# State @ w_in as three float32r passes on split weights, the limit on GpSimd, and another order of the first steps

## The chip, the cores and the metric

One core of one Trainium2 chip runs the whole program. The metric is the device time of one execution in microseconds (us), lower is better. A difference of 0.2% of this kernel, some 2.9 us, is about what its measurement can tell from no change.

## The reference, cut to what matters

```python
# attention between x (8, 8, 512, 64) and state (8, 8, 32, 64), per batch and head
a = softmax(scale * x @ state.T);  xread = a @ state          # 512 rows of a batch
a2 = softmax(scale * state @ x.T); sread = a2 @ x             # 32 rows of a batch
x = concat([xread, sread], rows).reshape(8 * 544, 512)
# first feed-forward, d_ff 2048
h = x @ w_in;  g = maximum(0.01 * h, h);  x = g @ w_out
# second feed-forward, d_ff 1536: silu(x @ w_gate) * (x @ w_val) @ w_out2
```

The weights reach the kernel as 64-bit floats, seen as pairs of 32-bit integers.

## The kernel before

`xread @ w_in` is never computed in that order. For each batch b and block g of 512 hidden columns the kernel makes `state @ w_in` once (32 state rows of each of 8 heads, in sw tiles) and multiplies by the softmax `a`. Exactness comes from splitting: a float32 value v is kept as h, v rounded to float32r (a ScalarE cast, `split_h`, L165), and l = v - h (a VectorE subtraction, `split_l`, L168). A product is then three float32r matmuls, l·h, h·l and h·h, added up in PSUM (`passes`, L437).

The work before the change lies in the first stage of the program, the start and batch 0 (j = 0). In it the 16 pieces of w_in, keys ("in", g, k), and 16 of w_out, keys ("out", f), are loaded (tile ws, 128x512 pairs) and turned into float32 by `convert`, a generator that is pumped one step for each letter c: scale (ScalarE, L214), low (ScalarE, L215), sign (VectorE, L216), limit (VectorE, L219), join (VectorE, L222) and add (VectorE, L225, tile raw or w_in). A piece of w_out is split afterwards into w_parts. A piece of w_in is kept in float32, unsplit, in the tile w_in, and also stored to DRAM.

Two functions use it:

- `product_sw` (L459, letter p): the states of four batches of two heads, `flat`, times one piece of w_in, one head on partitions 0 to 63 and one on 64 to 127, each into its own PSUM bank; ScalarE copies both banks to `sw` (L474) and SP stores them. There are 32 of these, all in the first stage. The letters of batch 0 use the two banks "a" and "b".
- `state_win` (L453, letter h and the steps "keep"): the states of batch 0, two pairs of heads from the tile `states`, into one bank (L456); it is split directly into swh and swl. There are 8.

Both are plain float32 matmuls, which the trace shows as two instructions each. `START` is the order of the first steps written as letters, `SLOT0` that of the 16 slots of batch 0. In a slot, `h_mm` makes a block of hidden columns (six matmuls ps_h), `h_act` its activation and split (hs, gh, gl), and `y_mm` twelve matmuls into ps_y with w_parts. `scores` (ps_s, L319) and the softmax steps (letters 0 and 1) stand in between. All engines run their instructions in the order in which the program issues them, and wait on one another through semaphores.

`place_states` (letters s and S) copies `flat` into the block layout `states` on ScalarE (L1239), batch 0 first, then batches 1 to 7.

Of the kernel before, what the change touches and what calls it, by code (L numbers as in the profile page):

```python
# [25 lines left out]
def kernel(  # L26
# [61 lines left out]

    LOADS = "xswxxwww"
    ORDER = "iiiioiiooiioiioioiioioioiooooooo"  # L90
    START = "spc0Scpccc0p0cpccpcc1ccchcc1cccpc1clcpp0hcccpclp1c01cpcmcc"
    SLOT0 = [
        "DcHcpAccccSYLpcZccc",
        "DcHcAcccpSYLpccZccc",
# [135 lines left out]
    def store(key):  # L230
        if key[0] == "in":
            nc.sync.dma_start(out=win_dram[key[1]][:, key[2], :], in_=raw[key])

    def convert(keys, room, prepare, load_next, finish=None):


        done, before, prev = None, None, None
        todo = list(keys)
        while todo or before or (finish and done):
            key = todo.pop(0) if todo and room(todo[0]) else None  # L240
            if not (key or before or (finish and done)):
# [12 lines left out]
            yield 0.42  # L254
            if key:
                ops["low"]()
                ops["sign"]()
            yield 0.42
            if prev:
                prev["join"]()  # L260
            yield 0.69
            if split:
                finish[1](done)
                ready.append(done)
            if prev:
                prev["add"]()
                load_next()
                if not finish or before[0] == "in":
                    ready.append(before)
                    store(before)  # L270
            yield 0.69
            done, before, prev = before, key, ops

# [173 lines left out]


    WO = {}
    products = []  # L450
    sw_ps, SW_raw, SW = {}, {}, {}

    def state_win(b, g, q, bank):  # L453
        ps = (ps_y if bank == "y" else ps_a).tile([P, 512], F32, tag=bank, name="ps_sw")
        for i in range(2):
            nc.tensor.matmul(  # L456
                ps[2 * NS * i:2 * NS * (i + 1)], lhsT=states[:, 2 * q + i, b, :], rhs=raw["in", g, 2 * q + i],
                start=True, stop=True,
            )  # L459
        return ps  # L460

    def product_sw(g, p, bs, banks):

        pool = ps_y if banks == "yy" else ps_a
        ps = [pool.tile([P, 512], F32, tag=tag, name="ps_sw") for tag in banks]
        for e in range(2):
            half = slice(D * e, D * (e + 1))
            nc.tensor.matmul(  # L468
                ps[e], lhsT=flat[half, p, 4 * bs:4 * bs + 4, :].rearrange("d b n -> d (b n)"),
                rhs=raw["in", g, p][half], start=True, stop=True,  # L470
            )
        staged = stage_sw()
        for e in range(2):
            nc.scalar.copy(staged[e], ps[e])  # L474

            r = slice(NS, P) if bs == 0 else slice(0, P)
            nc.sync.dma_start(out=sw_dram[bs][g][2 * p + e, r], in_=staged[e][r])
# [3 lines left out]
    def stage_sw():  # L481

        if not sw_stages:
            y, x = ab.tile([P, KD, S], F32, tag="yst", name="sw"), first1.tile([P, 2, 512], F32, tag="x_tail", name="sw")
            sw_stages[:] = [[y[:, 0], y[:, 1]], [y[:, 2], y[:, 3]], [x[:, 0], x[:, 1]]] + [
                [pool.tile([P, 512], F32, tag=tag, name="sw", bufs=2) for pool, tag in ((cv, "sw"), (xin, "xn"))]
                for _ in range(2)
            ]
        sw_stages.append(sw_stages.pop(0))
        return sw_stages[-1]  # L490
# [541 lines left out]
    with tc.manual_schedule():  # L1032
# [12 lines left out]
                    src = rows(w_out, key[1])  # L1045
                stage(key, src, cv)

        pair = [None]

        def place1(key):  # L1050

            if key[0] == "in":
                n, half = divmod(KD * key[1] + key[2], 2)
                if half == 0:
                    pair[0] = wres.tile([P, 2, 512], F32, tag=f"wr{n + NF1 // 2}", name="w_in")
                raw[key] = pair[0][:, half, :]
            else:
                raw[key] = cv.tile([P, 512], F32, tag="raw", name="raw", bufs=4)

        def finish1_h(key):  # L1060
            while any((KD * g + p) // 2 + NF1 // 2 == key[1] for g, p, _ in products):
                pump_products(1)
            t = wres.tile([P, 2, 512], F32R, tag=f"wr{key[1]}", name="w_parts")
            WO[key[1]] = (t[:, 0, :], t[:, 1, :])
            split_h(t[:, 0, :], raw[key])

        def finish1_l(key):
            split_l(WO[key[1]][1], raw.pop(key), WO[key[1]][0])


        keys2 = []
# [111 lines left out]
        def keep_steps(g, q):  # L1183
            def product():
                pump_until(("in", g, 2 * q + 1))
                keep_sw_h(g, q, state_win(0, g, q, "b"))

            return [{"P": [product]}, {"D": [lambda: keep_sw_l(g, q)], "cost": 0.6, "now": True}]

# [30 lines left out]
        keep = [(0, 0), (0, 1)]  # L1220
        low = list(keep)

        flat = cv.tile([P, NPAIR, B, NS], F32, name="flat")
# [12 lines left out]
        def place_states(some):  # L1236
            for e in range(2):
                half = slice(D * e, D * e + D)
                nc.scalar.copy(states[half, :, some, NS * e:NS * e + NS], flat[half, :, some])  # L1239

        background[0] = convert(keys1, lambda key: True, place1, next_load1, (finish1_h, finish1_l))

# [3 lines left out]
        for action in START:  # L1246
            if action in "01":
                step = [next(halves[int(action)], {})]
                for part in "DAPL":
                    run(step, part)  # L1250
            elif action == "p":
                pump_products(1, "yy")
            elif action == "h":
                keep_sw_h(*keep[0], state_win(0, *keep.pop(0), "y"))
            elif action == "l":
                keep_sw_l(*low.pop(0))
            elif action == "s":
                place_states(slice(0, 1))
            elif action == "S":
                place_states(slice(1, B))  # L1260
            elif action in "mM":
                f = "mM".index(action)
                if f not in firsts:
                    h_mm(0, f)
                    firsts[f] = h_act(0, f)
                next(firsts[f], None)
            else:
                pump(1)
# [2 lines left out]
                run([step], part)  # L1271
        for g, q in keep:
            pump_until(("in", g, 2 * q + 1))
            keep_sw_h(g, q, state_win(0, g, q, "y"))
        for g, q in low:
            keep_sw_l(g, q)
        for f in range(2):
# [215 lines left out]
```

## Time and profile before

| what | value |
|---|---|
| median of three runs | 1469.8 us (1468.29 to 1470.42) |
| the profiled execution | 1469.83 us, of which the span of its instructions is 1468.0 us |
| PE busy in the span | 98% |
| VectorE (DVE), ScalarE (ACT), GpSimd (POOL) busy in the span | 57%, 47%, 0% |
| PE busy in the first 42 us, and from 42 to 141 us | 27.39 us, 93.78 us |
| PE busy from 141 us on | 1323.15 of 1327 us |

A share of the whole span says little here: the change touches only the part up to about 141 us, where the 16 slots of batch 0 end. At 42 us the first ps_y matmul starts. Those two marks cut the trace into a head, the slots of batch 0, and the rest.

### The profile page before, as it was taken

The numbers are of one execution on the slowest core, as the hardware profiler recorded it, in microseconds if no ns is written. First come the engines' busy times: TensorE is split into PE (matmuls) and PEld (weight loads), VectorE is DVE, ScalarE is ACT, GpSimd is POOL, SyncE is SP. The second block draws the span as 40 slices with busy tenths as digits, with TensorE's granted clock in tenths as the row PEclk, the third lists the DMA queues.
The fourth block names the chain that finished last, engine by engine and source line by source line (L and its number), as shares of the span: only waits on it lengthen the run. The fifth ranks groups of instructions, "written<-read, shape, count | busy, mean of one in ns | idle before, by whom it ended". The sixth has DMA issues, their size and how long they took to land.

```text
span 1468.0 us, 20651 instructions
## 1 busy us (share of the span) xinstructions
PE 1444.3 (98%) x7530; PEld 1153.4 (79%) x7530; DVE 829.5 (57%) x1476; ACT 687.8 (47%) x1243; POOL 3.0 (0%) x8
## 2 busy tenths in 40 slices
PE   6999999999999999999999999999999999999998
PEld 1545777777777778888888888888888888988887
DVE  5877677677767676243454535555344655544442
ACT  6877656655655665454333433334233343333322
POOL 0000000000000000000000000000000000000000
PEclk8999999999999999999999999999999999999999
DMA  8895556665655656360668676667666397876345
GB/s 283 301 319 200 187 198 228 204 222 197 233 204 194 224 194 208 97 198 35 203 199 277 232 235 199 194 220 243 231 193 194 101 321 241 267 251 192 116 153 191
DMA packets 145764, 307.55 MB, mean 209 GB/s; under 512 B 14080, under 2 KB 34816, under 8 KB 144640
## 3 DMA queue, kind: packets, MB, share of 16 engines
q1 hardware_dynamic: 144368, 297.72, 61.7%
q10 hardware_dynamic: 1296, 8.52, 1.4%
q8 instruction: 60, 0.98, 0.3%
q14 instruction: 40, 0.33, 0.1%
HBM read 231.74 MB, written 74.45 MB: 209 GB/s over the span
## 4 chain that ended last, share of the span: by engine, by line
PE 97%; ACT 1%; DVE 1%; DMA 0%; issue 0%; SPq 0%; ACTq 0%
PE ps_y L444 24%; PE ps_o L444 19%; PE ps_x L742 18%; PE ps_h L444 14%; PE ps_s L742 9%; PE ps_a L742 4%; PE ps_sw L468 2%; PE ps_t L444 2%; PE ps_yt L444 2%; PE ps_s L319 1%; PE ps_r L416 1%; PE ps_sw L456 1%; PE ps_a L402 0%; ACT sw L474 0%; DMA flat<-in_dram 0%
## 5 line engine op out<-in xcount | busy, mean ns | idle before, releaser
L444 PE MATMUL ps_y<-gh,w_parts 128*128 128x512 f32 x1024 | 339.3, 391 | 0.0
L742 PE MATMUL ps_x<-yc,wq 128*128 128x512 f32 x1152 | 278.0, 389 | 0.0
L742 PEld LDWEIGHTS ps_x<-yc,wq 128*128 128x128 f32 x1152 | 216.2, 188 | 44.8
L444 PE MATMUL ps_o<-wo,zh 128*128 128x512 f32 x768 | 236.3, 389 | 0.0
L444 PEld LDWEIGHTS ps_y<-gh,w_parts 128*128 128x128 f32 x1024 | 192.2, 188 | 51.7 <-issue 7.6
L444 PE MATMUL ps_y<-gl,w_parts 128*128 128x512 f32 x512 | 199.4, 389 | 0.0
L168 DVE TENSOR_TENSOR gl<-hs,gh 128x512 fp32r<-128x512 f32 (+1 forms) x144 | 95.1, 661 | 141.6 <-ACT gh L165 141.4
L444 PEld LDWEIGHTS ps_o<-wo,zh 128*128 128x128 f32 x768 | 144.2, 188 | 29.8
L550 ACT ACTIVATE hs<-ps_h 128x512 f32<-128x512 f32 (+1 forms) x144 | 82.7, 574 | 172.4 <-PE ps_h L444 168.8
L444 PE MATMUL ps_o<-wo,zl 128*128 128x512 f32 x384 | 149.5, 389 | 0.1
L742 PE MATMUL ps_s<-yc,wq 128*128 128x512 f32 x576 | 146.1, 389 | 0.0
L168 DVE TENSOR_TENSOR zl<-z,zh 128x512 fp32r<-128x512 f32 x96 | 66.4, 691 | 114.6 <-ACT zh L165 114.6
L742 PEld LDWEIGHTS ps_s<-yc,wq 128*128 128x128 f32 x576 | 108.1, 188 | 22.4
L165 ACT CAST zh<-z 128x512 fp32r<-128x512 f32 x96 | 59.3, 622 | 140.7 <-PE ps_o L444 140.6
L762 ACT ACTIVATE sg<-C 128x512 f32<-128x512 f32 x72 | 45.5, 632 | 158.1 <-DVE C L758 158.1
L444 PEld LDWEIGHTS ps_y<-gl,w_parts 128*128 128x128 f32 x512 | 96.1, 188 | 19.6
L444 PE MATMUL ps_h<-ah,swl 128*128 128x512 f32 x256 | 106.3, 415 | 1.1 <-DVE swl L168 1.1
L758 DVE TENSOR_TENSOR C<-ps_s,C 128x512 f32<-128x512 f32 x48 | 33.2, 691 | 122.9 <-PE ps_s L742 122.9
L444 PE MATMUL ps_h<-al,swh 128*128 128x512 f32 x256 | 100.2, 391 | 0.2 <-DVE al L168 0.2
L754 ACT COPY C<-ps_x 128x512 f32<-128x512 f32 x96 | 55.9, 583 | 94.6 <-PE ps_x L742 94.6
L444 PE MATMUL ps_h<-ah,swh 128*128 128x512 f32 x256 | 100.2, 391 | 0.0
L165 ACT CAST gh<-hs 128x512 fp32r<-128x512 f32 (+1 forms) x144 | 85.7, 595 | 3.0
(129 smaller groups left out, 1912.8 us busy)
## 6 DMA issues: line engine op xcount, KB each, us to landing
wo<-wo SPq DMA_DIRECT2D x96, 512.0 KB
wq<-quad_gate SPq DMA_DIRECT2D x168, 256.0 KB
wq<-quad_val SPq DMA_DIRECT2D x168, 256.0 KB
ws<-in_dram SPq DMA_DIRECT2D x68, 512.0 KB
sw<-sw_dram SPq DMA_DIRECT2D x56, 256.0 KB
quad_gate<-hl SPq DMA_DIRECT2D x24, 512.0 KB
quad_val<-hl SPq DMA_DIRECT2D x24, 512.0 KB
yr<-y_dram SPq DMA_DIRECT2D x34, 256.0 KB
```

Of the source, the lines that this page charges most:

```text
L165: nc.scalar.copy(dst, src)
L168: nc.vector.tensor_tensor(out=dst, in0=src, in1=hi.bitcast(F32), op=ALU.subtract)
L319: nc.tensor.matmul(ps[2 * NS * i:2 * NS * (i + 1)], lhsT=states[:, p, b, :], rhs=xt.pop((b, p)), start=True, stop=True,)
L416: nc.tensor.matmul(ps[NS * k:NS * (k + 1), i], lhsT=v["et"][:, n:n + NS], rhs=tokens[i][:, c, NS * k:NS * (k + 1)], start=(c == 0), stop=( ...
L444: nc.tensor.matmul(ps, lhsT=w, rhs=v, start=first and n == 0, stop=last and n == len(todo) - 1)
L456: nc.tensor.matmul(ps[2 * NS * i:2 * NS * (i + 1)], lhsT=states[:, 2 * q + i, b, :], rhs=raw["in", g, 2 * q + i], start=True, stop=True,)
L468: nc.tensor.matmul(ps[e], lhsT=flat[half, p, 4 * bs:4 * bs + 4, :].rearrange("d b n -> d (b n)"), rhs=raw["in", g, p][half], start=True, s ...
L550: nc.scalar.activation(hs, ps[:, :n], AF.Prelu, alpha=0.01)
L742: nc.tensor.matmul(bank, lhsT=a, rhs=v, start=first and n == 0, stop=last and n == len(todo) - 1, skip_group_check=True,)
L754: nc.scalar.copy(t[0], src)
L758: nc.vector.tensor_tensor(out=kept[0], in0=bank, in1=kept[0], op=ALU.add)
L762: nc.scalar.activation(t[0], c, AF.Sigmoid)
```

## The change

Every piece of w_in is now split like w_out, into w_parts, a list `places` assigns it one of twelve places (tags wr4 to wr15, four of them used twice), and a place is overwritten only after all products of the piece in it have been issued (`clear`). The states are split as well: flat_h (ScalarE) and flat_l (VectorE), and for batch 0 first_h and first_l, block layouts filled by GpSimd copies. `product_sw` becomes three float32r passes, each for both heads in turn; `state_win` becomes six full-width passes. The limit of all but the first four pieces moves from VectorE to GpSimd. The copy of the states of batches 1 to 7 moves from ScalarE to GpSimd. A copy of a one-column tile `table` puts ScalarE's table load ahead of the first landing. sw copies have eight staging tiles rather than ten, since the tile x_tail now holds firsts_hl. START is another string; SLOT0 stays.

```diff
-    START = "spc0Scpccc0p0cpccpcc1ccchcc1cccpc1clcpp0hcccpclp1c01cpcmcc"
+    START = "sccccScc0ccc0cpccc10cpccpc1cpc0chc1chpc0lcp1l1mcpcpcc"
...
+        engine = nc.gpsimd if key[0] in ("in", "out") and key not in keys1[:4] else nc.vector
...
-            "limit": lambda: nc.vector.tensor_scalar(
+            "limit": lambda: engine.tensor_scalar(
                 out=hi_f, in0=hi_f, scalar1=HI_MAX, scalar2=-HI_MAX, op0=ALU.min, op1=ALU.max
...
-    def state_win(b, g, q, bank):
+    def state_win(g, q, bank):
+
         ps = (ps_y if bank == "y" else ps_a).tile([P, 512], F32, tag=bank, name="ps_sw")
-        for i in range(2):
-            nc.tensor.matmul(
-                ps[2 * NS * i:2 * NS * (i + 1)], lhsT=states[:, 2 * q + i, b, :], rhs=raw["in", g, 2 * q + i],
-                start=True, stop=True,
-            )
+        passes(
+            [((first_h[:, 2 * q + i], first_l[:, 2 * q + i]), WIN[g, 2 * q + i]) for i in range(2)], ps, True, True
+        )
+        kept.add((g, q))
         return ps
...
-        for e in range(2):
-            half = slice(D * e, D * (e + 1))
-            nc.tensor.matmul(
-                ps[e], lhsT=flat[half, p, 4 * bs:4 * bs + 4, :].rearrange("d b n -> d (b n)"),
-                rhs=raw["in", g, p][half], start=True, stop=True,
-            )
+        wh, wl = WIN[g, p]
+        for n, (st, w) in enumerate(((flat_l, wh), (flat_h, wl), (flat_h, wh))):
+            for e in range(2):
+                half = slice(D * e, D * (e + 1))
+                nc.tensor.matmul(
+                    ps[e], lhsT=st[half, p, 4 * bs:4 * bs + 4, :].rearrange("d b n -> d (b n)"), rhs=w[half],
+                    start=n == 0, stop=n == 2,
+                )
...
+        table = cv.tile([P, 1], F32, name="table")
+        nc.gpsimd.memset(table, 0.0)
+        nc.scalar.copy(table, table)
         nc.gpsimd.memset(states, 0.0)
+        nc.gpsimd.memset(firsts_hl.bitcast(F32), 0.0)
...
+        def split_states():
+            split_h(flat_h, flat)
+            split_l(flat_l, flat, flat_h)
+            for t, of in ((first_h, flat_h), (first_l, flat_l)):
+                for p in range(NPAIR):
+                    for e in range(2):
+                        half = slice(D * e, D * e + D)
+                        c = NS * (2 * (p % 2) + e)
+                        nc.gpsimd.tensor_copy(out=t[half, p, c:c + NS], in_=of[half, p, 0])
...
             elif action == "S":
-                place_states(slice(1, B))
+                split_states()
+                place_states(slice(1, B), nc.gpsimd.tensor_copy)
```

How the order of instructions moves, at three places.

On ScalarE, at the start of the program, before the change:

```order
L1239 ACT_TABLE_LOAD
L1239 COPY states<-flat 64x4x32 x2
L214 ACTIVATE ws<-ws 128x512
L327 COPY s<-ps_s 128x512
L1239 COPY states<-flat 64x4x7x32 x2
L215 ACTIVATE ws<-ws 128x512
L214 ACTIVATE ws<-ws 128x512
L344 ACTIVATE st<-st 128x512
```

and of the change, from the same place:

```order
L1252 ACT_TABLE_LOAD
L1252 COPY table<-table 128x1
L1260 COPY states<-flat 64x4x32 x2
L216 ACTIVATE ws<-ws 128x512
L217 ACTIVATE ws<-ws 128x512
L165 CAST flat_h<-flat 128x1024
L216 ACTIVATE ws<-ws 128x512
L217 ACTIVATE ws<-ws 128x512
L329 COPY s<-ps_s 128x512
L216 ACTIVATE ws<-ws 128x512
L165 CAST w_parts<-raw 128x512
L217 ACTIVATE ws<-ws 128x512
```

The table load no longer stands behind the states, the long states copy is gone, and the cast of flat and those of w_in stand in the row.

On VectorE, in a slot of batch 0 (sign, join, add and limit of two pieces, and the split of one), before:

```order
L216 TENSOR_SCALAR w_in<-ws 128x512
L222 SCALAR_TENSOR_TENSOR raw<-ws,raw 128x512
L168 TENSOR_TENSOR gl<-hs,gh 128x512
L225 ISA raw<-ws,raw 128x1024
L219 TENSOR_SCALAR ws<-ws 128x512
L216 TENSOR_SCALAR raw<-ws 128x512
L222 SCALAR_TENSOR_TENSOR w_in<-ws,w_in 128x512
L168 TENSOR_TENSOR w_parts<-raw,w_parts 128x512
```

and of the change, in a slot that does the same:

```order
L224 SCALAR_TENSOR_TENSOR raw<-ws,raw 128x512
L168 TENSOR_TENSOR w_parts<-raw,w_parts 128x512
L227 ISA raw<-ws,raw 128x1024
L168 TENSOR_TENSOR gl<-hs,gh 128x512
L218 TENSOR_SCALAR raw<-ws 128x512
L224 SCALAR_TENSOR_TENSOR raw<-ws,raw 128x512
L168 TENSOR_TENSOR w_parts<-raw,w_parts 128x512
L227 ISA raw<-ws,raw 128x1024
```

The limit is gone from VectorE's row, and every piece has a split where only those of w_out had one. The join now stands right behind the sign of the next piece.

On GpSimd, the whole program's work after its constants, of the change (before, only the memset of states, the two rows of ident and the last memset were there):

```order
L1251 MEMSET table 128x1
L1253 MEMSET states 128x2048
L1254 MEMSET firsts_hl 128x1024
masks.py:197 MEMSET ident 128x128
masks.py:199 ISA
masks.py:199 AFFINE_SELECT ident<-ident 128x128
L1270 COPY firsts_hl<-flat_h 64x32 x8
L1270 COPY firsts_hl<-flat_l 64x32 x8
L1260 COPY states<-flat 64x4x7x32 x2
L221 TENSOR_SCALAR ws<-ws 128x512 x28
L1383 MEMSET zero 128x512
```

18 copies and 28 limits have come to an engine that did no such work.

## Rows read from the trace of the kernel before

**Rows 1.** Windows, busy us of each engine, clock, DMA, of head, batch 0, rest.

```profile
0.00:42.00 42.00, 27.39 (x66) 9.55 (x66) 25.78 (x50) 27.52 (x49) 2.44 (x7) 0.84 0.80 276
42.00:141.00 99.00, 93.78 (x349) 50.17 (x348) 81.31 (x154) 80.74 (x151) 0.00 (x0) 1.00 0.85 289
141.00:1468.00 1327.00, 1323.15 (x7119) 1093.67 (x7117) 722.43 (x1273) 579.53 (x1045) 0.53 (x1) 1.00 0.61 201
```

**Rows 2.** Waits of PE from 42 to 141 us: total us, times, longest.

```profile
PE ps_sw L468 <- ACT sw L474: 3.5, 5, 0.8
PE ps_h L444 <- DVE swl L168: 1.1, 2, 0.5
```

**Rows 3.** Timeline of PE, one product, then one state_win, and matmuls around them.

```profile
43.26 0.40 PE L444 MATMUL ps_y<-gh,w_parts 128*128 128x512 f32 x1
43.59 1.13 PE L468 MATMUL ps_sw<-w_in,flat 64*128 64x512 f32 x4
44.65 0.50 PE L444 MATMUL ps_y<-gh,w_parts 128*128 128x512 f32 x1
44.98 0.39 PE L444 MATMUL ps_y<-gl,w_parts 128*128 128x512 f32 x1
...
73.46 0.39 PE L444 MATMUL ps_y<-gh,w_parts 128*128 128x512 f32 x1
73.78 1.08 PE L456 MATMUL ps_sw<-w_in,states 128*64 128x512 f32 x4
74.79 0.50 PE L444 MATMUL ps_h<-ah,swl 128*128 128x512 f32 x1
75.12 0.39 PE L444 MATMUL ps_h<-al,swh 128*128 128x512 f32 x1
75.36 0.39 PE L444 MATMUL ps_h<-ah,swh 128*128 128x512 f32 x1
75.59 0.40 PE L444 MATMUL ps_h<-ah,swl 128*128 128x512 f32 x1
```

**Rows 4.** Windows of 0.1 us inside one product, instructions of L468 alone.

```profile
41.30:41.40 0.10, 0.10 (x2) 0.00 (x0) 1.00 1.10 205
41.40:41.50 0.10, 0.10 (x4) 0.00 (x0) 1.00 0.62 102
41.70:41.80 0.10, 0.10 (x2) 0.00 (x0) 1.00 0.73 287
```

**Rows 5.** Groups from 42 to 141 us: count, busy us, mean ns, idle before.

```profile
L468 PE MATMUL ps_sw<-w_in,flat 64*128 64x512 f32 x98 | 31.1, 640 | 3.5 <-ACT sw L474 3.5
L219 DVE TENSOR_SCALAR ws<-ws 128x512 f32<-128x512 f32 x25 | 10.6, 423 | 0.0
L168 DVE TENSOR_TENSOR w_parts<-raw,w_parts 128x512 fp32r<-128x512 f32 x15 | 10.3, 684 | 0.0
L165 ACT CAST w_parts<-raw 128x512 fp32r<-128x512 f32 x15 | 9.3, 618 | 0.0
L456 PE MATMUL ps_sw<-w_in,states 128*64 128x512 f32 x24 | 7.2, 618 | 0.0
```

**Rows 6.** Chain that ended last in the first 60 us: start, us, what.

```profile
4.85 1.28 ACT L1239
...
10.37 0.83 ACT states L1239
11.21 0.94 ACT states L1239
...
36.76 0.70 DVE al L168
```

**Rows 7.** Timeline of GpSimd at the start of the program.

```profile
0.73 1.80 POOL L1233 MEMSET states<- 128x2048 f32 x1 [0.29 <-POOLq L1479]
2.47 0.20 POOL masks.py:197 MEMSET ident<- 128x128 f32 x1
2.75 0.29 POOL masks.py:199 TENSOR_SCALAR_AFFINE_SELECT ident<-ident 128x128 f32<-128x128 f32 x1
```

More of the change, by code (lines that the diff above doesn't have):

```diff
@@ L267, in convert @@
                 load_next()
-                if not finish or before[0] == "in":
+                store(before)
+                if not finish:
                     ready.append(before)
-                    store(before)
             yield 0.69
@@ L483, in stage_sw @@
         if not sw_stages:
-            y, x = ab.tile([P, KD, S], F32, tag="yst", name="sw"), first1.tile([P, 2, 512], F32, tag="x_tail", name="sw")
-            sw_stages[:] = [[y[:, 0], y[:, 1]], [y[:, 2], y[:, 3]], [x[:, 0], x[:, 1]]] + [
+            y = ab.tile([P, KD, S], F32, tag="yst", name="sw")
+            sw_stages[:] = [[y[:, 0], y[:, 1]], [y[:, 2], y[:, 3]]] + [
                 [pool.tile([P, 512], F32, tag=tag, name="sw", bufs=2) for pool, tag in ((cv, "sw"), (xin, "xn"))]
@@ L1046, in next_load1, with clear, finish1_h @@
                 stage(key, src, cv)
-        pair = [None]
         def place1(key):
-            if key[0] == "in":
[L1053 to L1064, printed above, removed]
+            raw[key] = cv.tile([P, 512], F32, tag="raw", name="raw", bufs=4)
+        places = [*range(4, 16), *range(12, 16)]
+        holds = {}
+        def clear(place):
+            one = holds.pop(place, None)
+            while one and any((g, p) == one for g, p, _ in products):
+                pump_products(1)
+            assert not one or (one[0], one[1] // 2) in kept, one
+        def finish1_h(key):
+            place = key[1] if key[0] == "out" else places[KD * key[1] + key[2]]
+            clear(place)
+            t = wres.tile([P, 2, 512], F32R, tag=f"wr{place}", name="w_parts")
+            if key[0] == "in":
+                holds[place] = key[1:]
+            (WIN if key[0] == "in" else WO)[key[1:] if key[0] == "in" else key[1]] = (t[:, 0, :], t[:, 1, :])
             split_h(t[:, 0, :], raw[key])
         def finish1_l(key):
-            split_l(WO[key[1]][1], raw.pop(key), WO[key[1]][0])
+            parts = WIN[key[1:]] if key[0] == "in" else WO[key[1]]
+            split_l(parts[1], raw.pop(key), parts[0])
         keys2 = []
@@ L1185, in product @@
                 pump_until(("in", g, 2 * q + 1))
-                keep_sw_h(g, q, state_win(0, g, q, "b"))
+                keep_sw_h(g, q, state_win(g, q, "b"))
             return [{"P": [product]}, {"D": [lambda: keep_sw_l(g, q)], "cost": 0.6, "now": True}]
@@ L1221 @@
         low = list(keep)
-        flat = cv.tile([P, NPAIR, B, NS], F32, name="flat")
+        flat = ab.tile([P, NPAIR, B, NS], F32, tag="ah1", name="flat")
+        flat_h, flat_l = (cv.tile([P, NPAIR, B, NS], F32R, name=f"flat_{t}") for t in "hl")
+        firsts_hl = first1.tile([P, 2, NPAIR, P], F32R, tag="x_tail", name="firsts_hl")
+        first_h, first_l = firsts_hl[:, 0], firsts_hl[:, 1]
         for action in LOADS:
@@ L1232, with place_states @@
                 )
+        table = cv.tile([P, 1], F32, name="table")
+        nc.gpsimd.memset(table, 0.0)
+        nc.scalar.copy(table, table)
         nc.gpsimd.memset(states, 0.0)
+        nc.gpsimd.memset(firsts_hl.bitcast(F32), 0.0)
         make_identity(nc, ident)
-        def place_states(some):
+        def place_states(some, copy):
             for e in range(2):
                 half = slice(D * e, D * e + D)
-                nc.scalar.copy(states[half, :, some, NS * e:NS * e + NS], flat[half, :, some])
+                copy(states[half, :, some, NS * e:NS * e + NS], flat[half, :, some])
+        def split_states():
[7 more added lines that the diff above has]
+                        nc.gpsimd.tensor_copy(out=t[half, p, c:c + NS], in_=of[half, p, 0])
         background[0] = convert(keys1, lambda key: True, place1, next_load1, (finish1_h, finish1_l))
@@ L1253 @@
             elif action == "h":
-                keep_sw_h(*keep[0], state_win(0, *keep.pop(0), "y"))
+                pump_until(("in", keep[0][0], 2 * keep[0][1] + 1))
+                keep_sw_h(*keep[0], state_win(*keep.pop(0), "y"))
             elif action == "l":
@@ L1257 @@
             elif action == "s":
-                place_states(slice(0, 1))
+                place_states(slice(0, 1), nc.scalar.copy)
             elif action == "S":
-                place_states(slice(1, B))
+                split_states()
+                place_states(slice(1, B), nc.gpsimd.tensor_copy)
             elif action in "mM":
@@ L1273 @@
             pump_until(("in", g, 2 * q + 1))
-            keep_sw_h(g, q, state_win(0, g, q, "y"))
+            keep_sw_h(g, q, state_win(g, q, "y"))
         for g, q in low:
```

2 lines of the change are left out of this document (added).

## The prediction

> **What bounds the kernel now.** I read three views, in this order. First the windows, cut at the two marks of the table, 42 us (the first ps_y) and 141 us (the end of batch 0). The reader is to see three regimes in the PE column. From 141 us on PE is busy 1323.15 of 1327 us, so whatever the change gains or loses before that mark is handed on one to one [rows 1]. From 42 to 141 us PE is busy 93.78 of 99.00 us, with VectorE at 81.31 and ScalarE at 80.74: PE is the bound, but two engines stand not far behind it [rows 1]. In the first 42 us PE is busy 27.39 us at a mean granted clock of 0.84, so some of that at the lower level, and nothing is near full: the head is a chain of single steps [rows 1]. Second, PE's waits in batch 0: they are 3.5 us in five waits of a product for the copies of the product before it, and 1.1 us for swl [rows 2]. So the slots are PE's own work plus a little more. Third, the chain in the head, which starts with ScalarE: a table load, then the copies of the states, and much later al on VectorE [rows 6].
>
> The sum below is made against the profiled execution's own 1469.83 us (span 1468.0 and 1.8 around it), which is the median of the runs too, 1469.8. What this kernel's measurement can tell from no change is 0.2%, 2.9 us.
>
> **Batch 0, work on PE.** A product shows as four instructions of 640 to 690 ns that fill only 1.13 us, so two run at a time; inside one product the count of running instructions goes 2, 4, 2, the second pair starting about 0.43 us after the first (the first starts shortly before 41.0 us, the second at about 41.4) [rows 3, 4, 5]. A full-width float32r pass follows the last one after 0.23 us (75.36 to 75.59) [rows 3]. The ps_y matmul before the product starts at 43.26 and the second after it at 44.98: 1.72 us for two passes and a product, so a product costs 1.72 - 2 x 0.23 = 1.26 us, of which two pair steps are 0.86 and 0.40 is getting in and out [rows 3]. The new product has three pair steps of 0.23, if float32r halves overlap as float32 halves do: 0.69 + 0.40 = 1.09 us, a gain of 0.17. The 98 instructions in this stretch are 24.5 products [rows 5]: 24.5 x 0.17 = -4.2 us. A state_win costs 75.12 - 73.46 - 0.46 = 1.20 us [rows 3]; six full-width passes cost 6 x 0.23 = 1.38, with nothing to get in and out of. That is +0.18 for each of the six here (24 instructions) [rows 5], +1.1 us. Sum on PE: **-3.1 us**. From below: if only the streaming mattered and the 0.40 shrank with it by a third, -6 us. From above: if halves don't overlap, the rival below.
>
> **Batch 0, the other engines.** Twelve pieces of w_in are split here that were not. ScalarE: 12 casts of 618 ns, +7.4 us, 80.74 to 88.2 [rows 1, 5]. VectorE: 12 subtractions of 684 ns, +8.2, less 25 limits of 423 ns, -10.6: 81.31 to 78.9 [rows 1, 5]. Against a stretch of 99.00 - 3.1 = 95.9 us both still have room, 7.7 and 17 us. This is the cover that I count on. If it is gone, the split and the cast cost up to their 7.4 us. Queued behind a late cast on ScalarE stand the two copies of a product, and PE waits for those with both banks full [rows 2]; the copies were already the largest wait.
>
> **The limit on GpSimd.** The trace shows no such instruction. Its memsets give 0.20 us for 128 columns and 1.80 for 2048, 0.83 ns a column, so 512 columns of a memset take 0.52 us; the select over 128 columns, which reads and writes, takes 0.29, and four of those are 1.16 us [rows 7]. I take 0.65, nearer to the memset, since both rows have a fixed part that four selects would count four times. GpSimd does nothing else in the slots [rows 1], a limit is issued as soon as its sign is done and the join that waits for it comes a piece later, so at 28 x 0.65 = 18 us in 130 its time itself is hidden. Cost zero, from 0 to what the rival on ports gives.
>
> **The head.** Removed: the table load from behind the landing of flat, -1.28 us, and the long copy of states from ScalarE, -1.77 us (0.83 + 0.94) [rows 6]. Together -3.05. Added to ScalarE is the cast of flat, 1024 columns, about two casts of 618 ns, 1.2 us [rows 5], of which some fits into what ScalarE has idle (27.52 busy of 42) [rows 1]. Added to VectorE up to its first gl, counted in its order: the split of flat, about 2 x 684 ns = 1.4, four more splits of pieces, 2.7, less three limits, -1.3; 2.8 us in all [rows 5]. VectorE is busy 25.78 of 42 us, and at least 10 us of the idle time lie after the table load's end at 6.13 [rows 1, 6], so some of the 2.8 falls into holes, but al at 36.76 shows VectorE on the chain at the end [rows 6]. I let 2.0 us of it land: -3.05 + 2.0 = **-1.0 us**. Bounds: -4 if all of it falls into holes and the products in the head, partly at the lower clock, give 1 us as well; +2.5 if all 2.8 land and the copies on GpSimd are late for the first state_win (16 of 32 columns at about 0.15 and two of 896 at 0.83 ns a column, some 4 us of work by the memset rows [rows 7]). SP's queue holds the same transfers in nearly the same order; the stores of w_in now read raw, one of four buffers that w_out's pieces share, which makes a piece wait for the store four pieces back. At some 3 us a piece I count that as hidden.
>
> Sum: 1469.8 - 3.1 - 1.0 = **1465.7 us**.
>
> **Rivals.**
>
> *The shared port makes VectorE the bound (slower).* If a GpSimd limit and VectorE's join, add and splits exclude each other, each limit takes its own length from VectorE, where it took 0.42 us before. With 25 in batch 0, VectorE's 78.9 us becomes 78.9 + 25 t: at 0.52 us 91.9, at 0.65 95.2, at 1.16 107.9, against PE's 95.9 [rows 1, 5, 7]. It decides from t = 0.68 on. At 1.0 us: 103.9, so +8.0 on the forecast, 1473.8; I take **1474**. For it: the join stands right behind a sign in VectorE's row, just when the freed limit starts. Against it: VectorE has transposes, reductions and idle time in which a limit costs nothing. The Trainium skill, SBUF — State Buffer, section "Who interferes with whom", says that a VectorE instruction with two SBUF inputs contends with a GpSimd one that reads SBUF, and that the loser fully blocks; by that rule this rival's mechanism is sure and only t is open. No run here shows it, since GpSimd is idle whenever VectorE works.
>
> *ScalarE eats PE's gain (same).* With 7.7 us of slack left and strict order, the copies of a product come later. If each of 24.5 products waits 0.13 us more, PE's 3.1 us are gone and **1469** remains: the gain moves into waits of ps_sw for sw. For it: this wait exists already [rows 2]. Against it: ScalarE spends 18 us idle in batch 0 now [rows 1].
>
> *The halves don't overlap in float32r (slower).* Then six passes in a row: 6 x 0.23 + 0.40 = 1.78, +0.52 for each of 24.5, +12.7 and +1.1 - 1.0: **1483**. The pairs of float32 overlap plainly [rows 4], which speaks against it.
>
> *The head gives all it can (faster).* -4 in place of -1: **1462.7**, and with a cheaper way in and out of the products 1460.
>
> **How the numbers follow.** Forecast 0.41, port 0.19, ScalarE 0.27, no overlap 0.05, all of the head 0.08. The range runs to the port case with a little more and to the last one: 1461.5 to 1476, which leaves out the no-overlap case, the far end of the port case and the last microsecond of the best. Where the forecast itself holds, 1463 to 1467.5. Faster by over 0.2% (below 1466.9): 0.41 and 0.08, less a little at the edge, 0.48. Within: the ScalarE case and the edge, 0.27. Slower (above 1472.7): 0.25.
>
> **What would show it.** Right: products in batch 0 as six instructions within some 0.95 us, state_win about 1.4 us, PE's waits there still 4 to 6 us, batch 0 about 96 us from the first ps_y on, and that ps_y at about 41 us. VectorE's join and add should keep 690 ns: if they stretch, or if many begin late behind GpSimd, the port rival is true. PE waiting for sw or for swl more than 8 us in batch 0 would mean ScalarE. A first ps_y after 43 us would make the head's term wrong, and a product of 1.5 us or more the overlap.

## The result, and the profile after

The changed kernel takes 1489.8 us (median of 4 runs, 1488.6 to 1491.2) against 1469.9 us before (4 runs, 1468.3 to 1470.4): a ratio of 1.0137, interval 1.0125 to 1.015. It is 20 us slower, where 4 us faster was forecast. The profiled execution took 1488.6 us, its span 1486.8.

The windows of the changed kernel, cut near the same marks as [rows 1] (columns: PE, PEld, VectorE, ScalarE and GpSimd busy, clock, DMA):

```profile
0.00:42.00 42.00, 27.69 (x68) 12.86 (x68) 28.64 (x49) 24.59 (x45) 15.13 (x30) 1.00 0.71 247
42.00:160.00 118.00, 102.52 (x429) 65.99 (x428) 89.51 (x143) 91.77 (x171) 24.84 (x25) 0.96 0.75 252
160.00:1486.80 1326.80, 1322.81 (x7117) 1093.36 (x7115) 722.27 (x1274) 579.40 (x1044) 0.52 (x1) 1.00 0.62 202
```

From the end of batch 0 on, PE is busy 1322.81 us, as in [rows 1]: the loss lies ahead of that. To divide it I use two marks that every trace here has: the first ps_y matmul, and the first copy of a finished ps_y, which closes batch 0 (in the kernel before it stands 13 us behind the 141 us of [rows 1], where the 16 slots end). What lies between is called the slots. Before, the marks are at 42.0 and 154.0 us; after, at 46.1 and 172.6. So the head lost 4.1 us, and the slots grew from 112.0 to 126.5, by 14.5. The windows of the slots, before:

```profile
42.00:154.00 112.00, 106.78 (x406) 60.95 (x405) 85.20 (x160) 86.57 (x161) 0.00 (x0) 1.00 0.80 269
```

and after:

```profile
46.10:172.60 126.50, 111.02 (x467) 73.75 (x465) 92.89 (x148) 93.63 (x175) 24.19 (x24) 0.96 0.72 239
```

PE's idle time went from 112.00 - 106.78 = 5.2 us to 126.50 - 111.02 = 15.5. PE's busy time rose too, by 4.2 us, though by the forecast its work shrank: the clock is 0.96 there, and 4% of 126.5 us are 5 us, by estimate. VectorE's rises by 7.7, where a fall of 2.4 was counted. ScalarE and VectorE are each idle for over 32 us of these slots, so neither is full.

PE's waits in the slots after, to be held against [rows 2] (total, times, longest):

```profile
PE ps_sw L474 <- ACT sw L480: 10.1, 7, 3.5
PE ps_sw L446 <- ACT sw L480: 2.0, 2, 1.0
PE ps_h L446 <- DVE swl L168: 1.4, 2, 0.7
```

and ScalarE's own waits there:

```profile
ACT hs L556 <- PE ps_h L446: 9.3, 5, 2.3
ACT swh L165 <- PE ps_sw L446: 7.2, 4, 3.2
ACT sw L480 <- PE ps_sw L474: 6.8, 10, 2.6
ACT w_parts L165 <- DVE raw L227: 6.4, 7, 1.8
```

PE waits for the copies of products on ScalarE, which stand behind a cast, which waits for VectorE's add. That last row is new: before, the casts of w_parts had an idle time of 0.0 ahead of them [rows 5]. Neither loads nor the eight staging tiles show as a cause: in these slots ScalarE waits 0.7 us for a load, and its copies to sw never wait for a store.

One such chain in the timeline after, from 115.5 to 120 us (start, length, engine, what, idle before and for whom):

```profile
115.56 0.60 ACT L556 ACTIVATE hs<-ps_h 128x512 f32<-128x512 f32 x1
115.70 0.69 DVE L336 TENSOR_REDUCE m<-st 128x16 f32<-128x512 f32 x1
116.04 0.69 ACT L216 ACTIVATE ws<-ws 128x512 f32<-128x512 f32 x1
116.31 0.68 DVE L224 SCALAR_TENSOR_TENSOR raw<-ws,raw 128x512 int32<-128x512 int32 x1
...
116.91 0.68 DVE L168 TENSOR_TENSOR w_parts<-raw,w_parts 128x512 fp32r<-128x512 f32 x1
...
117.51 0.68 DVE L227 CUSTOM_DVE_ANT_0 raw<-ws,raw 128x1024 uint16<-128x1024 uint16 x1
...
118.22 0.62 ACT L165 CAST w_parts<-raw 128x512 fp32r<-128x512 f32 x1 [1.50 <-DVE raw L227]
118.45 0.68 DVE L224 SCALAR_TENSOR_TENSOR raw<-ws,raw 128x512 int32<-128x512 int32 x1
118.61 1.02 POOL L221 TENSOR_SCALAR ws<-ws 128x512 f32<-128x512 f32 x1 [2.82 <-DVE raw L218]
118.75 1.07 ACT L480 COPY sw<-ps_sw 128x512 f32<-128x512 f32 x2
119.05 1.13 DVE L168 TENSOR_TENSOR w_parts<-raw,w_parts 128x512 fp32r<-128x512 f32 x1
...
119.38 0.98 PE L474 MATMUL ps_sw<-w_parts,flat_l 64*128 64x512 f32 x2 [3.52 <-ACT sw L480]
```

ScalarE has the product's copies ready to run, but the cast ahead of them sits 1.50 us until the add has ended; PE then starts after 3.52 idle us. The 1.50 are a part of these; the rest is what stands ahead of the copies in ScalarE's row anyway (hs, a scale, the cast itself). The add is late because VectorE runs without a pause: a reduction of the softmax, the join and the split of the piece before stand ahead of it. The price doesn't end there. The windows of 4 us after, around two such stalls, show the clock:

```profile
58.00:62.00 4.00, 1.81 (x9) 0.96 (x8) 1.87 (x3) 2.24 (x5) 0.72 (x1) 1.00 0.64 251
62.00:66.00 4.00, 4.00 (x14) 2.69 (x10) 3.95 (x7) 2.87 (x7) 1.22 (x2) 0.59 0.79 260
...
114.00:118.00 4.00, 1.86 (x11) 0.93 (x9) 3.34 (x6) 2.73 (x6) 0.66 (x1) 1.00 0.89 305
118.00:122.00 4.00, 2.62 (x9) 1.72 (x10) 3.38 (x6) 3.77 (x8) 1.02 (x1) 0.84 0.79 268
```

PE was busy 1.81 of 4 us, and the next 4 us ran at a mean granted clock of 0.59, most of them at the lower level (1.2 GHz); the same follows at 118 us, less strongly. Before, on the same grid, no window in the slots has PE under 3.17 busy, and all have a clock of 1.00; the lowest is:

```profile
62.00:66.00 4.00, 3.17 (x13) 1.63 (x12) 2.85 (x6) 3.67 (x8) 0.00 (x0) 1.00 0.87 306
```

The product and the state_win that were costed show in PE's timeline, answering to [rows 3]:

```profile
44.91 0.39 PE L446 MATMUL ps_h<-ah,swh 128*128 128x512 f32 x1
45.23 0.50 PE L474 MATMUL ps_sw<-w_parts,flat_l 64*128 64x512 f32 x2
45.56 0.63 PE L474 MATMUL ps_sw<-w_parts,flat_h 64*128 64x512 f32 x4
46.12 0.50 PE L446 MATMUL ps_y<-gh,w_parts 128*128 128x512 f32 x1
46.46 0.48 PE L446 MATMUL ps_y<-gl,w_parts 128*128 128x512 f32 x1
...
125.17 1.52 PE L446 MATMUL ps_sw<-w_parts,firsts_hl 128*128 128x512 f32 x6
126.53 0.39 PE L446 MATMUL ps_h<-ah,swl 128*128 128x512 f32 x1
```

From 44.91 to 46.46 are 1.55 us, less 2 x 0.23 for two passes 1.09: the very number of the forecast. A state_win that nothing holds up takes 126.53 - 125.17 = 1.36, where 1.38 was forecast.

The groups of the slots after, answering to [rows 5] (count, busy, mean ns, idle before):

```profile
L168 DVE TENSOR_TENSOR w_parts<-raw,w_parts 128x512 fp32r<-128x512 f32 x27 | 27.5, 1017 | 3.5 <-ACT w_parts L165 3.5
L221 POOL TENSOR_SCALAR ws<-ws 128x512 f32<-128x512 f32 x24 | 24.2, 1008 | 76.3 <-DVE raw L218 67.4 <-ACT sw L480 8.9
L224 DVE SCALAR_TENSOR_TENSOR raw<-ws,raw 128x512 int32<-128x512 int32 x26 | 17.7, 682 | 0.0
L227 DVE CUSTOM_DVE_ANT_0 raw<-ws,raw 128x1024 uint16<-128x1024 uint16 x26 | 17.7, 679 | 0.0
L165 ACT CAST w_parts<-raw 128x512 fp32r<-128x512 f32 x26 | 16.1, 620 | 6.4 <-DVE raw L227 6.4
```

The split on VectorE takes 1017 ns where it took 684, in a kernel with limits on GpSimd; join and add keep their 680. The port rival was therefore true as a mechanism, and was the first thing to test.

### The profile page after: what moved, and what is told of

The parts are those of the page before. It is cut to its first block, busy times and chain, and to the rows that moved or that the text cites. A ratio compares the mean times of both kernels' runs of the same rounds, so it can differ in the third digit from the quotient of the medians.

```text
span 1486.8 us, 20946 instructions
## 1 busy us (share of the span) xinstructions
PE 1453.0 (98%) x7610; PEld 1172.2 (79%) x7610; DVE 840.4 (57%) x1465; ACT 695.8 (47%) x1259; POOL 40.5 (3%) x56
## 4 chain that ended last, share of the span: by engine, by line
PE 91%; issue 3%; ACT 2%; DVE 2%; DMA 2%; POOL 0%; SPq 0%; ACTq 0%; POOLq 0%
PE ps_y L446 22%; PE ps_o L446 18%; PE ps_x L748 18%; PE ps_h L446 13%; PE ps_s L748 9%; PE ps_a L748 4%; PE ps_t L446 2%; PE ps_yt L446 2%; PE ps_s L321 1%; ACT sw L480 1%; PE ps_r L418 1%; PE ps_sw L474 1%; DMA ws<-in_dram 1%; DMA wo<-wo 0%; PE ps_a L404 0%
```

## The experiments

Each run was timed beside runs of the kernel before on the same chip; "before +" and "after +" say which kernel is edited.

### First round: the parts of the change that looked guilty

**e1_limit_vector**, after + the limit back on VectorE.

```diff
-        engine = nc.gpsimd if key[0] in ("in", "out") and key not in keys1[:4] else nc.vector
+        engine = nc.vector
```

> The changed kernel with all 32 limits back on VectorE, everything else as changed. Theory port (limits on GpSimd, 981 ns each, hold up VectorE's splits, whose mean is 978 ns in place of 684, some 0.45 us each time for 20 of 27, and that is what the slots lose): the stretches go, about 9 us, but 28 limits come back on VectorE at 0.34 to 0.42 us, 9.5 to 12 us, so about 1489, within 3 us of the changed kernel; the splits are back at 684 ns. Theory ScalarE (the twelve to sixteen added casts, each behind an add of VectorE and ahead of the copies of a product, set the pace): about 1490 as well or somewhat above, with PE's wait for sw still 8 us or more. A result below 1480 would mean that the stretch costs far more than its own length.

Measured: 1488.7 us, ratio 1.0125 (1.011 to 1.014). The splits are back at 685 ns, and PE still waits 9.3 us for the copies of products. Moving the limits off GpSimd gives their work back to VectorE, and the sum is nothing that can be told apart.

**e2_no_limit**, after + the 28 limits on GpSimd left out altogether.

> The changed kernel without the 28 limits of GpSimd (that clamp is left out; the four on VectorE stay). Nothing replaces them, so this is all that the limits cost where they are now. Theory port: the 9 to 10 us of stretched splits are gone and the wait of join for limit too: 1478 to 1481. Theory ScalarE: VectorE gains 9 us that it spends waiting for ScalarE: 1485 to 1488.

Measured: 1486.8 us, 1.0115 (1.0098 to 1.0132). Limit and port together are worth 3 us of 20.

**e3_before_limit_gpsimd**, before + the change's `engine = ...` line, so that only the limit moves.

> The kernel before with one part of the change alone: the limits of all but the first four pieces on GpSimd. Theory port: VectorE saves 28 x 0.34 = 9.5 us and loses 0.45 us for each join or split that meets a limit, 7 to 12 us; no change, 1468 to 1473. Theory ScalarE: the same, since VectorE isn't the bound: 1467 to 1470. A result of 1475 or more would mean that the move alone is a large part of the loss.

Measured: 1470.8 us, 1.0008 (0.9998 to 1.0018), no change. In the kernel before, moving the limits costs nothing.

**e5_copies_off_gpsimd**, after + the states' copies of batches 1 to 7 on ScalarE, and firsts_hl filled by eight VectorE copies.

> The changed kernel with the copies of the start off GpSimd: the long states copy on ScalarE as before, and the 16 copies into firsts_hl as 8 on VectorE. The head lost 4.1 us (first ps_y at 46.12 in place of 42.01 us). Theory head-by-GpSimd (the 18 copies took from 8.6 to 18.5 us and stretched VectorE's sign and join to 1.15 and 1.41 us): some 2 us come back, 1487 to 1488. Theory head-by-queue (SP stands from 32.8 to 42.6 us before stores of sw that wait for ScalarE's copies, and the next piece's load is issued only at 42.7): within 1 us of the changed kernel, as the queue stays.

Measured: 1490.0 us, 1.0133 (1.0116 to 1.0149); first ps_y at 46.8 us rather than 46.1. GpSimd's copies take 9.8 us in a row, but done elsewhere they don't bring the head back.

**g3_start_before**, after + the START of before.

> The changed kernel with START as it was before. Theory order (the new START delays the first ps_y by 4 us and sets up the queue that stands until 42.7 us): 3 to 5 us faster than the changed kernel, 1484 to 1487. Theory dependency (the products now need a split that comes four steps after the add, so the old order, written for products right after the add, waits more): slower than the changed kernel, 1490 to 1500.

Measured: 1491.5 us, 1.0142 (1.0127 to 1.0157). First ps_y moves from 46.1 to 51.6 us, and the slots shrink by 2.4: the new START helps the head of the changed kernel by 5.5 us, and part of that is handed back in the slots. The total differs by 1.6 us, less than can be told from no change.

### Second round: one part of the split at a time

**g1_before_cast**, before + a cast of each finished piece of w_in, into a tile that nobody reads, at the place where the change casts.

```diff
+            extra = finish and done and done[0] == "in"
+            if extra:
+                both = cv.tile([P, 2, 512], F32R, tag="both", name="both", bufs=1)
+                split_h(both[:, 0, :], raw[done])
             if prev:
                 prev["limit"]()
```

> The kernel before with one thing added: each finished piece of w_in is also cast by ScalarE into a scratch tile that nobody reads, in the row where the change casts it (16 casts of 618 ns, behind VectorE's add, ahead of the next piece's scale). The products stay float32. Theory ScalarE (the added casts, each waiting for an add of VectorE in ScalarE's strict order, hold up the copies of the products): 6 to 12 us slower, 1476 to 1482. Rival (the pace is lost on PE itself or in the order of the start, not by the casts): within 3 us of before, 1470 to 1473.

Measured: 1479.8 us, 1.0065 (1.005 to 1.008). Sixteen casts of 0.6 us that nothing depends on cost 9.5 us, about half of the whole loss. In the slots PE's wait for sw is back, and the cast's wait for the add with it; waits of PE and of ScalarE:

```profile
PE ps_sw L472 <- ACT sw L478: 8.3, 6, 2.9
...
ACT both L165 <- DVE w_in L225: 3.4, 2, 2.0
```

**g2_before_split**, g1 + the subtraction, as unused.

```diff
             yield 0.69
+            if extra:
+                split_l(both[:, 1, :], raw[done], both[:, 0, :])
```

> As the one before, and VectorE also subtracts (16 of 684 ns into the other half of the scratch tile): the whole splitting of w_in without any use of it, limits on VectorE. Theory ScalarE and VectorE coupled: the larger part of the change's 20 us, 1480 to 1488. Rival: 1470 to 1475.

Measured: 1482.4 us, 1.0081 (1.0066 to 1.0096). The subtraction adds 2.6 us to the cast's 9.5, which is just within what can be told from no change; 7.4 us remain to the change.

**g4_cast_gpsimd**, after + limits on VectorE, and twelve casts of w_in on GpSimd.

> The changed kernel with all limits on VectorE and the casts of 12 pieces of w_in on GpSimd in place of ScalarE. Theory ScalarE: its 7.4 us of added work in the slots are gone, but the split now waits for GpSimd, which takes 1 us: 1478 to 1484. Rival (ScalarE's load is not what counts): 1487 to 1493.

Measured: 1487.0 us, 1.0107 (1.009 to 1.0124). ScalarE's busy time in the slots falls to 86.7 us of 124.0, a smaller share than before the change (86.6 of 112.0), and only 2.8 us come back. ScalarE's load alone is not it. The casts of w_out, the only pieces left to it in these slots, now wait 5.5 us for the add.

**h2_after_copies_shared** and **h5_before_copies_shared**, after and before + every second copy of a product on VectorE, the neighbour with more idle time.

```diff
-            nc.scalar.copy(staged[e], ps[e])
+            if e == 0:
+                nc.scalar.copy(staged[e], ps[e])
+            else:
+                nc.vector.tensor_copy(out=staged[e], in_=ps[e])
```

> The changed kernel with the second of a product's two sw copies on VectorE (692 ns there by the rows that read PSUM, 590 on ScalarE). Theory load on ScalarE: its added casts, 16 of about 0.55 us, are more than paid by 32 copies less, so most of the slots' loss comes back although VectorE gets 32 x 0.69 = 22 us: 1476 to 1483. Rival (both engines are equally full, VectorE's splits hold the row up): 1487 to 1496.

> The kernel before with the second of a product's two sw copies on VectorE, nothing else. Theory load on ScalarE (the copies are what PE waits for, 4.4 us in the first stage, and ScalarE runs near 78 to 80 percent busy whatever it is given): 2 to 5 us faster than before, 1465 to 1468. Rival (VectorE, at 81 of 99 us, is as near its limit): 1470 to 1480.

Measured: 1499.1 us, 1.0202 (1.0187 to 1.0217), and 1485.2 us, 1.0105 (1.009 to 1.012): misses. Relief for ScalarE makes both kernels slower by 9 and 15 us. That is the opposite of what a theory of ScalarE's load asks for. (VectorE gets 14 us more to do in the slots of h5, 99.2 for 85.2, so load on VectorE isn't excluded by it.) A product's two banks are then free only when two engines have each come to them in their order, which would explain it, but no run shows that apart.

**h3_after_no_low**, after + no low half of w_in: sixteen subtractions, one of a product's three passes and two of a state_win's six left out.

> The changed kernel without the low half of w_in: its 16 subtractions on VectorE and the pass with it, one of three, are left out, and the products need only ScalarE's cast. Theory load on ScalarE: VectorE and PE have less to do but the casts stay, 4 to 7 us faster than the changed kernel, 1483 to 1486. Rival (the split and the wait for it are the main part): 1474 to 1480.

Measured: 1480.1 us, 1.0072 (1.0055 to 1.0089). First ps_y is back at 42.5 us, and the slots are still 122.2 long: the low half sets the change's head, and most of the loss in the slots stays without it.

### Third round: load or order

**h1_before_cast_ready**, g1 with the same sixteen casts from a tile that was finished long ago.

```diff
-                split_h(both[:, 0, :], raw[done])
+                split_h(both[:, 0, :], states[:, 0].rearrange("p b n -> p (b n)"))
```

> The kernel before with the 16 added casts of 618 ns in the same places of ScalarE's row, but from a tile that has long been written, so that no cast waits for VectorE (they do nothing useful). Theory load (16 more instructions in ScalarE's strict order delay what stands behind them, whatever they read): as slow as with the casts of the finished pieces, 1477 to 1481. Rival coupling (the wait for the add is what costs, 3.9 us of it in that run): 1470 to 1474.

Measured: 1472.1 us, 1.0017 (1.0008 to 1.0027). The same work at the same place costs 2.4 us rather than 9.5 when it has nothing to wait for. Here the theory of load falls as the main cause. It keeps a part: the slots of h1,

```profile
41.30:156.70 115.40, 107.09 (x406) 61.26 (x405) 85.85 (x160) 92.20 (x173) 0.00 (x0) 1.00 0.78 260
```

are 3.4 us longer than before and PE is idle for 8.3 us there rather than 5.2, at a clock of 1.00, while the first ps_y comes 0.7 us sooner.

**i1_before_cast_late**, g1 with the cast, of the right data, two parts of the step later: behind the step's low and whatever ScalarE has to do in between, ahead of the next add.

```diff
             if prev:
                 prev["join"]()
+            if extra:
+                split_h(both[:, 0, :], raw[done])
             yield 0.69
```

> The kernel before with the 16 added casts of the finished pieces of w_in, read by nobody, but issued two steps of the conversion later, behind low and sign and ahead of join, when VectorE's add lies well back. Theory coupling (a cast right behind the add and one scale makes ScalarE wait for VectorE in strict order, and VectorE's next sign for ScalarE): most of the 9.5 us of the early cast is gone, 1471 to 1474, like the casts of a ready tile (1472.12). Rival (reading the piece at all costs, because it holds up what overwrites or stores it): 1477 to 1481 again.

Measured: 1471.3 us, 1.0008 (0.9999 to 1.0018). The 9.5 us have become 1.5, within what can be told from no change. The windows of the slots, in g1:

```profile
41.30:162.00 120.70, 109.81 (x406) 62.66 (x405) 85.83 (x160) 92.31 (x173) 0.00 (x0) 0.97 0.75 249
```

and in i1:

```profile
42.10:155.70 113.60, 107.71 (x407) 61.08 (x406) 85.49 (x160) 91.83 (x174) 0.00 (x0) 1.00 0.80 264
```

VectorE and ScalarE do the same work in both (85.8 and 85.5, 92.3 and 91.8 us); the slots differ by 7.1 us, PE's idle time by 10.9 against 5.9, and the clock by 0.97 against 1.00. Only the cast's place in ScalarE's row is different. Of the 7.1 us, 5.0 are idle time of PE and 2.1 its busy time.

**i2_after_split_late**, after + that order: the cast ahead of the join, the subtraction behind the next add.

```diff
             split = finish and done in raw and done not in ready
-            if split:
-                finish[0](done)
             if prev:
                 prev["limit"]()
...
             yield 0.42
+            if split:
+                finish[0](done)
             if prev:
                 prev["join"]()
             yield 0.69
+            if prev:
+                prev["add"]()
             if split:
                 finish[1](done)
                 ready.append(done)
             if prev:
-                prev["add"]()
                 load_next()
```

> The changed kernel with the cast of a finished piece two conversion steps later (ahead of join) and its subtraction behind the next add, for w_in and w_out alike; all work stays. Theory coupling: ScalarE's wait for add (9.1 us) goes and the slots lose less, 5 to 9 us faster than the changed kernel, 1481 to 1485. Rival (the products' own dependence on the split is what costs): they now start two steps later, 1489 to 1496.

Measured: 1483.5 us, 1.0091 (1.0076 to 1.0106): 6.3 us of the 20 come back, with cast and subtraction of w_in and w_out both moved. The cast's wait for the add is gone from ScalarE's list, and PE's wait for sw falls from 10.1 to 5.5 us.

**i4_before_split_late**, before + the same edit, where only w_out is split.

> The kernel before with the same shift of cast and subtraction for the pieces of w_out alone. Theory coupling: ScalarE waits for add only 0.4 us there as it stands, so little to win, 1468 to 1470.5; rival: y waits for w_parts later, 1471 to 1474.

Measured: 1469.8 us, 0.9999 (0.999 to 1.0008). With half the pieces split the old order costs nothing.

**h4_before_table**, before + the copy of `table`, which puts the table load ahead.

> The kernel before with one part of the change alone: the copy of a one-column tile that pulls ScalarE's table load (1.28 us) ahead of the landing of flat. My head's term: the load stands first on the head's chain, so up to 1.3 us faster, 1468.5. Rival: the head hands nothing on, since later steps wait for loads and VectorE, 1469.5 to 1470.5.

Measured: 1469.4 us, 0.9998 (0.9988 to 1.0007). PE in its timeline, where before the first scores are one row from 6.85 to 9.75:

```profile
5.73 1.94 PE L319 MATMUL ps_s<-xt,states 128*64 128x512 f32 x2 [5.73 <-ACT states L1242]
8.11 1.63 PE L319 MATMUL ps_s<-xt,states 128*64 128x512 f32 x2 [0.44 <-DMA xt<-in_dram]
```

The scores begin 1.1 us earlier, and the second pair then waits for the landing of xt, and ends at 9.74: the gain is gone at once.

**j1_before_split_late**, before + the whole split of w_in, late and unused.

> The kernel before with the whole split of w_in, cast and subtraction, in the late places and used by nobody; products float32, limits on VectorE. It costs ScalarE 16 casts and VectorE 16 subtractions without a single new wait for a product. Theory coupling and dependence (the work itself fits into idle time; what costs is who waits for it): 1472 to 1475. Rival (VectorE's added 11 us are simply too much): 1478 to 1483.

Measured: 1475.5 us, 1.0038 (1.0023 to 1.0052), slightly over the expectation. First ps_y is at 46.4 us, and the slots are 113.4 long: in good order the split is nearly free in the slots (1.4 us) and costs its time in the head (4.4).

**j2_after_late_no_limit**, i2 + the 28 limits left out.

> The changed kernel with the late split, and without the 28 limits of GpSimd (the clamp is left out). Port's share once ScalarE no longer waits for add: VectorE's splits go from about 980 back to 684 ns. Theory port small: 0 to 4 us faster than with the late split alone, 1480 to 1483. Rival (the port was hidden behind the coupling): 1472 to 1478.

Measured: 1481.7 us, 1.0083 (1.0068 to 1.0098): 1.75 us better than i2, 2.1 in the slots; the intervals overlap, so this is not clear of noise.

## Why the prediction was wrong, by its own steps

The marks of the traces sort the 18.6 us by which batch 0 ends later in the profiled executions (PE idle is the slots less PE's busy time):

| kernel | first ps_y | slots | PE idle in them |
|---|---|---|---|
| before | 42.0 | 112.0 | 5.2 |
| j1: before, split of w_in late and unused | 46.4 | 113.4 | 5.7 |
| j2: after, split late, no limits on GpSimd | 47.8 | 118.4 | 9.7 |
| i2: after, split late | 46.9 | 120.5 | 9.6 |
| after | 46.1 | 126.5 | 15.5 |

From the bottom up, the slots give 6.0 us for the place of cast and subtraction, 2.1 for the limits on GpSimd, 5.0 between j1 and j2, and 1.4 for the split in good order; the head gives 4.1 (the late order of i2 puts 0.8 more into it, so the slots' 6.0 are 5.2 at the end of batch 0).

**"Batch 0, the other engines", cost 0: this is the step that failed.** It counted 12 casts and 12 subtractions against the idle time of both engines, saw 7.7 and 17 us of it left, and called that idle time "the cover that I count on". ScalarE's load came out as counted (+7.1 us in the slots, for 7.4). VectorE's rose by 7.7 where a fall of 2.4 was counted, because its splits take 1017 ns beside the limits; without the limits it is 83.8 us, 1.4 less than before, and the loss is still 17 us (e2). So the load is not what failed, and both engines are idle for longer than before. But idle time is room only for an instruction that can run when it stands first in the row. The cast follows the add, the last thing that VectorE does in a step, and behind the cast stand the copies that free a product's banks. So a late add holds up ScalarE, then PE, and PE's longer pauses are followed by stretches at the lower clock. That order more than load does it is shown twice with unused casts, by h1 (ready data, 2.4 in place of 9.5 us) and i1 (another place, 1.5), and once in the change itself, by i2, for 6.3 of its 20 us. The rest of the 20 isn't shown to come from this wait.

**Rival "ScalarE eats PE's gain".** It named the right engine, the right wait and the sign that would show it ("PE waiting for sw or for swl more than 8 us in batch 0": it was over 10), but priced it at 0.13 us for each product, as a loss that would just eat PE's 3.1 us. That price failed: the longest of these waits is 3.5 us, and the clock comes on top.

**PE's term, -3.1 us: right in size, in part by luck.** A product takes 1.09 us as forecast, so float32r halves overlap, and that rival is out. The split of that number was misread, though. In [rows 3] the old product runs from 43.59 to 44.65 us, so its two pair steps are 0.53 each, not 0.43, and getting in and out is 0.20, not 0.40; the new one runs from 45.23 to 46.12, three steps of 0.30, not 0.23. The two errors cancel. The gain can't be seen in the total: j2 has 1.0 us more of PE busy time than j1 while 3% of its 118.4 us, some 3.6 us, go to the lower clock, so by estimate about 2.5 us of work less. The gain arrived where PE no longer set the pace.

**The limit on GpSimd, cost 0, and the port rival, 1474.** A limit takes 0.66 us beside a transpose (at 115.13 us) or a reduction (at 34.37), the 0.65 of the estimate. Most start about 0.16 us after a join: the join keeps its 0.68, the limit takes 1.02, and the split behind the join 1.13 in place of 0.68. Where no split follows (at 86.78 and 91.01 us) the limit still takes 1.03, so it is the join that lengthens it. The rule cited with the rival, in the Trainium skill, SBUF — State Buffer, section "Who interferes with whom", agrees in kind: what is lengthened stands beside an instruction with two SBUF inputs, and 0.36 us for the limit and 0.45 for the split are what taking turns would give; the runs don't show the turns themselves. But VectorE did not become the bound. The price was 3 us without the late order (e2), 1.75 and not clear of noise with it (j2), and none in the kernel before (e3).

**The head, -1.0 us: wrong sign, +4.1.** Of its parts, the table load's -1.28 is worth 0, since the landing of xt is late next (h4), which the term did not name. The states' long copy, put back on ScalarE with the other copies moved too, changes nothing that the time shows (e5). The 2.8 us on VectorE, of which 2.0 were let land, land in full and more: without the low half first ps_y is 3.6 us earlier (h3), and in the kernel before the split alone puts it 4.4 later (j1), the cast alone 0.1 (i1), so the subtractions do it. The order of START, which the sum doesn't price by itself, hides more: with the old one first ps_y would come at 51.6 (g3). "A first ps_y after 43 us would make the head's term wrong": it came at 46.1.

**What stays open.** The 5.0 us between j1 and j2 were not taken apart. The two differ in the use of the split pieces, where a product can't start until cast and subtraction are done, but also in START, the states' copies and the limits, which j1 still has on VectorE. In j2's slots PE waits 1.7 us for w_parts, all ahead of state_win's passes, and 5.7 for sw against 3.5 in j1, at a clock of 0.97; that these make up the 5.0 is argued from the waits only, and START is a rival: with the old one the changed kernel's slots are 2.4 us shorter (g3). Why the casts of w_out didn't find the add unfinished in the kernel before [rows 5] is not settled either. Their place doesn't spare them as such, since in g4 and h5 they wait 5.5 and 3.2 us for it; i4 shows that moving them in the kernel before gains nothing. No version here beats the kernel before; i4, h4, e3 and i1 can't be told from it.

## What to carry to other kernels

Idle time in an in-order engine is cover only for work whose input is ready when its turn comes; for each added instruction ask which engine produces its input, how late, and what stands behind it in the row. Where a step crosses from one engine to another and back, put the crossing a step later than it could be, and test that with a dummy before building on it: sixteen unused casts told more here than the whole profile. It was worth 8 us for those casts and 6 in the change, and nothing for the casts of w_out in the kernel before. And a pause of PE has to be priced with the clock that follows it, not by its length alone.

## What the runs showed of the hardware that was not expected

- Pauses and clock: after the two stalls shown (PE busy 1.81 and 1.86 of 4 us), the next 4 us ran at a mean clock of 0.59 and 0.84; in the slots of e1 the mean is 0.93, and PE is busy 113.1 us there, against 106.8 before at 1.00.
- A limit of 128x512 on GpSimd takes 0.66 us beside a transpose or a reduction on VectorE and 1.02 when it starts inside a join there; the join keeps its 0.68, and the split behind it goes from 0.68 to 1.13. Neither engine simply wins. The copies of 64x32 there take 0.37 to 0.48 us each, where 0.15 was estimated from memsets.
- Sharing two copies of one product between ScalarE and VectorE costs 15 us in the kernel before, more than any other edit that was made to it.
